# Low parts of a split-float kernel made by VectorE alone behind attention, instead of by VectorE and GpSimd

## The chip, the core and the metric

The kernel runs on one core of a Trainium2 chip. Its time is the device time in microseconds of one execution; three runs of the kernel before gave 2046.16, 2047.84 and 2050.9 us, a median of 2047.84 us. The engines are named as in the profile: PE (TensorE), PEld (its weight load), DVE (VectorE), ACT (ScalarE), POOL (GpSimd) and SP (SyncE, which issues most DMAs).

## The reference

Three stages follow each other. The input is q, k, v of 4 batches x 8 heads x 576 positions x 64 features.

```python
# attention with an exponential feature map
def phi(x):
    proj = np.einsum('bhsd,df->bhsf', x, w_phi)
    proj = proj - np.max(np.abs(proj), axis=-1, keepdims=True)
    return np.concatenate([np.exp(proj), np.exp(-proj)], axis=-1)
...
# first gated layer, 2304 tokens x 512
a = x @ w1; b = x @ w2
x = (a * b @ w3) @ w_out
...
# eight experts, every token goes through all of them
P = np.exp(logits)
for _ in range(8):
    P /= P.sum(1, keepdims=True) + 1e-09
    P /= P.sum(0, keepdims=True) + 1e-09
    P *= N / E
for e in range(E):
    h = np.maximum(x @ w1[e], 0.0)
    out += P[:, e:e + 1] * (h @ w2[e])
```

## The kernel before, in words

**Split numbers.** Every product of the two dense stages is made of three matmuls. Each operand is split into a high part (a copy in the type fp32r, mostly by ACT, `copy`, L96) and a low part (the number minus its high part, `subtract`, L99). `mm3` (L86) then issues high x high, high x low and low x high into one bank of PSUM; L87, L88 and L89 are these three matmuls. So every weight and every activation needs one low part, an elementwise subtraction of two tensors in SBUF.

**Which engine makes which part.** The table `ENG` (L13) gives a letter per step: a is ACT, v DVE, g POOL. A string of several letters is walked through by an index. `Wl="vgg"` (low parts of the experts' w1) has three pieces per tile: the first, 1024 columns wide, goes to DVE, the second (256 columns) and the third (512) to POOL. `W2l="vg"` sends the low parts of w2 to DVE for even units and to POOL for odd ones. `ol="vvvg"` sends two of the eight low parts of the product w3 w_out to POOL. `Xs="gv"` sends the sums of the first 768 columns of X to POOL and those of later columns to DVE. The low part of c = a*b (L717) is written out as a POOL instruction.

**Stages.** Attention takes the first 240 us or so. Then the gated layer runs over six column blocks j of 384 tokens: for each of eight row tiles ft it makes a and b (tiles ab), their product (L715), its high part cH on ACT (L716) and its low part cL (L717), and then four products px with w3 w_out. In the first block (j = 0) the weights w1 and w2 are also rebuilt from 64-bit words (L637 to L646) and split. Between the blocks DVE makes sums of expert weights ahead of time (`sum_next`, `sum_make`, L468).

**The experts.** They run over three super-columns s of 768 tokens. In the first (s = 0) each of the eight experts e has four units (p = 0 to 3) of `unit` (L851): seven products of six matmuls each, in the order a11, s2, s3, s1, a22, a12, s4 (`products`, L819). After each product DVE adds the PSUM bank into the running sums c (L836; ACT copies the first, L834). Five banks are in turn. A unit ends in two `h_split` (L812): hH by ACT, hL by DVE (L815). After the four units come six output tiles py of 24 matmuls (L942), which need all eight hH and hL, and a gated sum on DVE (L956, L958). The weights of the next unit are split meanwhile (`prep_w1`, L529), w2 of this unit behind it (`split_w2`, L792), and for experts 3 to 6 the sums of w2 are made (`sums_w2`, L806). In s = 1 and 2 the split weights are read back from DRAM, and no step of the change occurs there.

**Sinkhorn.** The gate's P is normalised eight times by rows and columns (`sinkhorn_rows`, L881, and `sinkhorn_cols`, L889), in small DVE instructions L883 to L897 and one matmul per round (cs, L891). `between` (L905) issues these steps behind the products of expert 0, so both DVE and PE carry them in their queues between other work.

**What sets the order.** Each engine works through its own queue in order and waits at the head of it. The order in the queues is chosen when the program is built: instructions get priorities (`tc.high_priority(60)` for the adds L836 and for the last h_split), and a scheduler places what is ready by its own idea of durations. Where a step changes its engine, the order of both engines, and of PE behind them, can change.

Of the kernel before, what the change touches and what calls it, by code (L numbers as in the profile page):

```python
# [11 lines left out]

ENG = dict(  # L13
    kh="a", num="a", rc="ga", xmul="gvgg", xh="a", xl="ggvg", woh="a",
    wol="g", w3h="a", w3l="g", w34="aaav", wh="av", wl="v", oh="va", ol="vvvg", Xh="a",
    Xl="v", Xs="gv", Wt="v", Wh="a", Wl="vgg", W2h="a", W2l="vg", Tw="v", Th="a", Tl="v",
)
AF = mybir.ActivationFunctionType
ALU = mybir.AluOpType
# [3 lines left out]
def f32(ap):  # L23
    return ap.bitcast(F32)
# [3 lines left out]
def kernel(  # L28
# [17 lines left out]
    nc = tc.nc  # L46
# [32 lines left out]
    def x_at(p, kt, c0, n):  # L79
        i, o = divmod(c0, NH)  # L80
        return XHL[i][p][:, kt, o : o + n]
# [4 lines left out]
    def mm3(ps, aH, aL, bH, bL, start, stop):  # L86
        nc.tensor.matmul(ps, aH, bH, start=start, stop=False)  # L87
        nc.tensor.matmul(ps, aH, bL, start=False, stop=False)  # L88
        return nc.tensor.matmul(ps, aL, bH, start=False, stop=stop).ins  # L89
# [418 lines left out]
    def load_w1(u):  # L508
        if u < len(units):
            s, e, p = units[u]  # L510
            if s > 0:
                return
            rawW1[u] = rw1.tile([P, 7, 2 * P], F32, name=f"r1_{u}", tag="r")
            nc.sync.dma_start(rawW1[u][:, 4:7], moe2_w1[e, p][:, 1:4])
            nc.sync.dma_start(rawW1[u][:, 0:4], W1T[u])
# [13 lines left out]
    def prep_w1(u):  # L529
        if u >= len(W1S):  # L530
            return
        r = rawW1.pop(u)
        hb, ha = w1_tiles(u)
        for i, (t, c, o) in enumerate(((ha, slice(0, 4), 0), (ha, slice(4, 5), 0), (hb, slice(5, 7), 5))):
            d = slice(c.start - o, c.stop - o)
            copy("Wh", t[:, 0, d], r[:, c], i)
            subtract("Wl", t[:, 1, d], r[:, c], f32(t[:, 0, d]), i)
        for t, d in zip((hb, ha), W1S[u]):
            nc.sync.dma_start(d, f32(t))
# [7 lines left out]
    def sbuf(c, name, bufs=1, side="right"):  # L547
        return c.enter_context(tc.tile_pool(name=name, bufs=bufs, side=side, reuse_waits="tile"))
# [28 lines left out]
    def sum_load(n):  # L577
        if n < len(jobs):
            kind, k = jobs[n]
            rawT[n] = tq[0].tile([P, 4, 2 * P], F32, name=f"tr{n}", tag="tr", bufs=3)  # L580
            if kind == "w1":
                nc.sync.dma_start(rawT[n], moe2_w1[k // NP, k % NP])
            else:
                nc.sync.dma_start(rawT[n].rearrange("p (j h) d -> p j h d", j=2), w2_rows(*k))
# [20 lines left out]
    def sum_next(behind):  # L605
        if made[0] < len(jobs):
            with tc.issue_after(behind):
                sum_make(made[0])
            made[0] += 1

    with ExitStack() as c2:
# [13 lines left out]
        w34 = {}  # L625

        def get_w12(n):
            ft, w = divmod(n, 2)
            if n < NW:
                t = W12E[n]  # L630
            else:
                r = rb.tile([P, DF], U32, name=f"rw{n}", tag="r")
                nc.sync.dma_start(r, w12i[ft][:, w * DM : (w + 1) * DM].bitcast(U32))
                r = r.rearrange("p (n x) -> p n x", x=2)
                t = st2.tile([P, DM], F32, name=f"w{n}", tag="wr")
                u = t.bitcast(U32)
                nc.scalar.activation(t, r[:, :, 1].bitcast(F32), AF.Copy, scale=2.0**-112)  # L637
                nc.vector.tensor_scalar(
                    u, u, 3, 0x7FFFFFFF, ALU.logical_shift_left, ALU.bitwise_and
                )  # L640
                nc.vector.scalar_tensor_tensor(
                    u, r[:, :, 0], 29, u, ALU.logical_shift_right, ALU.bitwise_or
                )
                nc.vector.scalar_tensor_tensor(
                    u, r[:, :, 1], 0x80000000, u, ALU.bitwise_and, ALU.bitwise_or
                )  # L646
            pool = w12a if ft == 0 else w12p
            hi = pool.tile([P, KT, P], F32R, name=f"wH{n}")
            lo = pool.tile([P, KT, P], F32R, name=f"wL{n}")
            t = t.rearrange("p (k f) -> p k f", k=KT)  # L650
            copy("wh", hi, t, n)
            subtract("wl", lo, t, f32(hi), n)
            w12[n] = hi, lo

        def get_w34(i):
            t = st2.tile([P, DM], F32, name=f"wo{i}", tag="wr")
            nc.sync.dma_start(t, W34[i // 2][:, i % 2])
            hi = w34p.tile([P, DM], F32R, name=f"woH{i}")
            lo = w34p.tile([P, DM], F32R, name=f"woL{i}")
            copy("oh", hi, t, i)  # L660
            subtract("ol", lo, t, f32(hi), i)
            w34[i] = hi, lo
# [30 lines left out]
        for j in range(NT // N1):  # L693
            c0 = j * N1
            for ft in range(FT):
                ab = []
                for w in range(2):
                    n = 2 * ft + w
                    if j == 0:
                        for i in range(3) if n == 0 else ():  # L700
                            get_w12(i)
                        if n + 3 < 2 * FT:
                            get_w12(n + 3)
                        if n >= FT:
                            get_w34(n - FT)
                    ps = ab_p.tile([P, N1], F32, name=f"ab{j}_{ft}_{w}", tag="ab")
                    hi, lo = w12[n]
                    for kt in range(KT):
                        mm3(ps, hi[:, kt], lo[:, kt], x_at(0, kt, c0, N1), x_at(1, kt, c0, N1), kt == 0, kt == KT - 1)
                    ab.append(ps)  # L710
                a_sb = ct.tile([P, N1], F32, name=f"a{j}_{ft}", tag="a")
                nc.scalar.copy(a_sb, ab[0])
                h, l = cH[ft], cL[ft]
                cc = a_sb
                behind = nc.vector.tensor_tensor(cc, ab[1], a_sb, ALU.mult).ins  # L715
                nc.scalar.copy(h, cc)  # L716
                nc.gpsimd.tensor_tensor(l, cc, f32(h), ALU.subtract)  # L717
                if 0 < j and (ft < FT - 1 if c0 + N1 < NT else ft % 2 == 0):
                    sum_next(behind)
            if c0 + N1 == NT:  # L720
                assert made[0] == len(jobs)
                c7.close()
                c3.close()
                xt_p.append(sbuf(c2, "xt6", KT))
                xc = sbuf(c4, "xc", side="left")
                wc1 = sbuf(c4, "wc1", 2, "left")
                c6 = c4.enter_context(ExitStack())
                rw1 = sbuf(c6, "rw1", 2, "left")
                wc1c = []
                load_w1(0)  # L730
                load_w1(1)
                prep_x(0)
                prep_w1(0)
            for dt in range(KT):
                ps = px_p.tile([P, N1], F32, name=f"px{j}_{dt}", tag="px")
                dc = slice(dt * P, (dt + 1) * P)
                for ft in range(FT):
                    hi, lo = w34[ft]
                    mm3(ps, hi[:, dc], lo[:, dc], cH[ft], cL[ft], ft == 0, ft == FT - 1)
                xt = xt_p[-1].tile([P, N1], F32, name=f"xt{j}_{dt}", tag="xt")  # L740
                nc.scalar.copy(xt, ps)
                i, o = divmod(c0, 2 * N1)
                nc.sync.dma_start(XS[i][:, dt, o : o + N1], xt)
                xh, xl = x_at(0, dt, c0, N1), x_at(1, dt, c0, N1)
                nc.scalar.copy(xh, xt)
                behind = nc.vector.tensor_tensor(xl, xt, f32(xh), ALU.subtract).ins
                if 0 < j < NT // N1 - 1:
                    sum_next(behind)
            if c0 < NH:
                logits([j])  # L750
            elif c0 + N1 == NT:
                logits(range(NH // N1, NT // N1))
            if j == 0:
                c5.close()
                tq.append(sbuf(c7, "tq", 2))
                for k in range(3):
                    sum_load(k)
            if c0 + N1 == NH:
                cx[0].close()
                rx = sbuf(c4, "rx", side="left")  # L760
                load_x(0)
# [5 lines left out]
    with c4:  # L767
# [238 lines left out]
        for u, (s, e, p) in enumerate(units):  # L1006
# [15 lines left out]
            a = [a01[:, lo_], a01[:, hi_], a2d[:, lo_]]  # L1022
# [135 lines left out]
```

## Time and profile before

| | us |
|---|---|
| median of three runs | 2047.84 |
| the profiled execution's own time | 2048.16 |
| its span, first to last instruction | 2046.4 |
| PE busy | 1994.6 (97%) |
| DVE busy | 1430.8 (70%) |
| ACT busy | 777.5 (38%) |
| POOL busy, 260 instructions | 297.2 (15%) |

The time lies 1.8 us above the span. PE's busy time is made of spans whose ends are modelled: a matmul of 384 columns has a span of some 340 ns, while the next one starts 0.17 to 0.18 us after it. So PE counts as idle only where the gap between two starts is longer than that span, and a busy share of 97% does not say that PE is at its peak. DVE's instructions overlap a little in the same way. POOL is busy until about 1050 us and idle behind it.

### The profile page before, as it was taken

The page shows a single profiled execution, that of the slowest core. Times are in us where ns is not written, and L with a number is a line of the kernel's source. Part 1 is how long each engine was busy: PE and PEld are TensorE (multiplying, and loading weights), DVE is VectorE, ACT ScalarE, POOL GpSimd, SP SyncE. Part 2 cuts the span into 40 slices and gives each one's busy share as a digit, 9 for nine tenths or more (in the row PEclk, how much of TensorE's full clock was granted, in tenths as well). Part 3 has the DMA queues.
Part 4 walks back from the last instruction along what each step waited for, and adds up shares of the span by engine and source line. Part 5 has one row for each costly group of instructions (what it writes and reads, how often), then busy time and mean ns, then how long its engine had stood idle before and what let it go on. Part 6 is the DMA issues. An engine that isn't in the chain of part 4 may idle for free.

```text
span 2046.4 us, 34054 instructions
## 1 busy us (share of the span) xinstructions
PE 1994.6 (97%) x13605; PEld 1865.1 (91%) x13605; DVE 1430.8 (70%) x2320; ACT 777.5 (38%) x1435; POOL 297.2 (15%) x260
## 2 busy tenths in 40 slices
PE   7899999999989999999999999999999999999999
PEld 6677789999988888888889999999999999999999
DVE  7766766666686459766776666777768677776666
ACT  6666532323433224332343333343334334333333
POOL 3433321121322223312220000000000000000000
PEclk9999999999999999999999999999999999999999
DMA  6433248788587668988976666666668666666664
GB/s 213 143 135 117 92 136 264 269 291 279 189 306 277 242 263 287 323 310 299 336 285 226 250 246 246 248 250 248 243 252 309 247 245 251 250 241 250 249 252 150
DMA packets 155502, 496.79 MB, mean 243 GB/s; under 512 B 12624, under 2 KB 73936, under 8 KB 128464
## 3 DMA queue, kind: packets, MB, share of 16 engines
q1 hardware_dynamic: 154752, 493.96, 67.5%
q8 instruction: 107, 1.75, 0.3%
q10 hardware_dynamic: 592, 0.66, 0.1%
q14 instruction: 51, 0.42, 0.1%
HBM read 348.82 MB, written 145.75 MB: 242 GB/s over the span
## 4 chain that ended last, share of the span: by engine, by line
PE 77%; DVE 9%; ACT 4%; issue 4%; DMA 3%; POOL 3%; SPq 0%; ACTq 0%; POOLq 0%; DVEq 0%
PE ps L87 5%; PE ps L89 5%; PE ps L88 5%; PE py L89 4%; PE pa L87 4%; PE pa L88 4%; PE pa L89 4%; PE py L88 4%; PE py L87 4%; PE b L1041 3%; PE b L1040 3%; PE b L1039 3%; PE ab L89 2%; PE ab L87 2%; PE ab L88 2%
## 5 line engine op out<-in xcount | busy, mean ns | idle before, releaser
L836 DVE TENSOR_TENSOR c<-c,ps 128x384 f32<-128x384 f32 x480 | 255.3, 547 | 58.3 <-PE ps L89 53.7
L834 ACT COPY c<-pa 128x384 f32<-128x384 f32 x96 | 45.7, 476 | 360.4 <-PE pa L89 321.8
L89 PE MATMUL py<-w,hL 128*128 128x512 f32 x384 | 153.8, 401 | 2.4 <-DVE hL L815 2.4
L87 PE MATMUL py<-w,hH 128*128 128x512 f32 x384 | 152.5, 397 | 2.9 <-ACT hH L814 2.8
L88 PE MATMUL py<-w,hH 128*128 128x512 f32 x384 | 152.4, 397 | 0.0
L1058 DVE SCALAR_TENSOR_TENSOR o<-mt,Pw,o 128x512 f32<-128x512 f32 x84 | 58.3, 747 | 122.7 <-ACT mt L1048 122.7
L99 POOL TENSOR_TENSOR w<-r,w 128x256 fp32r<-128x256 f32 x64 | 93.1, 1469 | 342.7 <-ACT w L96 307.9
L87 PE MATMUL ab<-XH,wH 128*128 128x384 f32 x384 | 131.3, 342 | 4.2 <-DVE wH L96 2.2
L89 PE MATMUL ab<-XH,wL 128*128 128x384 f32 x384 | 131.2, 342 | 1.5 <-DVE wL L99 1.5
L88 PE MATMUL ab<-XL,wH 128*128 128x384 f32 x384 | 130.4, 340 | 0.0
L958 DVE SCALAR_TENSOR_TENSOR o<-py,Pw,o 128x512 f32<-128x512 f32 x42 | 31.4, 748 | 125.8 <-PE py L89 125.8
L836 DVE TENSOR_TENSOR c<-c,pa 128x384 f32<-128x384 f32 x192 | 102.8, 548 | 9.8 <-PE pa L89 8.8
L1039 PE MATMUL b<-t,dh 128*128 128x256 f32 x384 | 108.7, 283 | 0.0
L1040 PE MATMUL b<-t,dh 128*128 128x256 f32 x384 | 108.7, 283 | 0.0
L1041 PE MATMUL b<-t,dl 128*128 128x256 f32 x384 | 108.7, 283 | 0.0
L89 PEld LDWEIGHTS py<-w,hL 128*128 128x128 f32 x384 | 72.2, 188 | 24.4 <-DVE hL L815 7.6
L993 ACT ACTIVATE c<-c 128x384 f32<-128x384 f32 x64 | 33.6, 526 | 156.1 <-DVE c L836 156.1
L87 PEld LDWEIGHTS py<-w,hH 128*128 128x128 f32 x384 | 72.4, 188 | 21.2 <-ACT hH L814 4.7
L717 POOL TENSOR_TENSOR cL<-a,cH 128x384 fp32r<-128x384 f32 x48 | 56.8, 1183 | 231.2 <-ACT cH L716 231.2
L88 PEld LDWEIGHTS py<-w,hH 128*128 128x128 f32 x384 | 72.3, 188 | 17.2 <-DVE w L99 0.3
L815 DVE SCALAR_TENSOR_TENSOR hL<-c,hH 128x768 fp32r<-128x768 f32 x64 | 79.8, 1254 | 3.1 <-ACT hH L814 2.5
L96 ACT CAST w<-r 128x512 fp32r<-128x512 f32 (+2 forms) x96 | 61.9, 686 | 45.4 <-issue 31.5
(266 smaller groups left out, 6493.7 us busy)
## 6 DMA issues: line engine op xcount, KB each, us to landing
t<-w2s SPq DMA_DIRECT2D x112, 1024.0 KB, 4.7
w<-w1s SPq DMA_DIRECT2D x64, 1280.0 KB, 5.5
w1s<-w SPq DMA_DIRECT2D x32, 1280.0 KB, 7.4
w<-w1s SPq DMA_DIRECT2D x64, 512.0 KB, 5.0
tr<-in_moe_w_dram SPq DMA_DIRECT2D x48, 512.0 KB, 5.4
w2s<-w SPq DMA_DIRECT2D x96, 256.0 KB, 4.3
w1t<-tt SPq DMA_DIRECT2D x32, 512.0 KB, 6.2
r<-w1t SPq DMA_DIRECT2D x32, 512.0 KB, 7.3
```

Source lines behind the costliest of these rows:

```text
L87: nc.tensor.matmul(ps, aH, bH, start=start, stop=False)
L88: nc.tensor.matmul(ps, aH, bL, start=False, stop=False)
L89: return nc.tensor.matmul(ps, aL, bH, start=False, stop=stop).ins
L96: (e.copy if e is nc.scalar else e.tensor_copy)(out, src)
L99: engine(key, i).tensor_tensor(out, a, b, ALU.subtract)
L717: nc.gpsimd.tensor_tensor(l, cc, f32(h), ALU.subtract)
L815: nc.vector.scalar_tensor_tensor(hL[ft], src, 0.0, f32(hH[ft]), ALU.max, ALU.subtract)
L836: nc.vector.tensor_tensor(o, t, ps, ALU.add)
L1039: nc.tensor.matmul(dst[i], H[:, c], T[:, 0], start=f, stop=False, skip_group_check=True)
L1040: nc.tensor.matmul(dst[i], H[:, c], T[:, 1], start=False, stop=False, skip_group_check=True)
L1041: nc.tensor.matmul(dst[i], L[:, c], T[:, 0], start=False, stop=l, skip_group_check=True)
L1058: nc.vector.scalar_tensor_tensor(o, src[i], w, o, ALU.mult, ALU.add)
```

## The change

Five strings of `ENG` lose their letter g, and the low part of c (L717) is issued on DVE. Nothing else is edited; no operation is added or left out, and the operands stay the same.

```diff
-    wol="g", w3h="a", w3l="g", w34="aaav", wh="av", wl="v", oh="va", ol="vvvg", Xh="a",
-    Xl="v", Xs="gv", Wt="v", Wh="a", Wl="vgg", W2h="a", W2l="vg", Tw="v", Th="a", Tl="v",
+    wol="g", w3h="a", w3l="g", w34="aaav", wh="av", wl="v", oh="va", ol="v", Xh="a",
+    Xl="v", Xs="v", Wt="v", Wh="a", Wl="v", W2h="a", W2l="v", Tw="v", Th="a", Tl="v",
...
-                nc.gpsimd.tensor_tensor(l, cc, f32(h), ALU.subtract)
+                nc.vector.tensor_tensor(l, cc, f32(h), ALU.subtract)
```

What moves from POOL to DVE: 48 low parts of c (384 columns each), 32 pieces of w1 of 512 and 32 of 256 columns, 16 low parts of w2 (1024 columns), 2 low parts of w3 w_out (512 columns) and the 4 sums of the first X (768 columns): 134 instructions. What POOL does in attention stays.

The first place is DVE's queue in the third and fourth unit of expert 4 (units 18 and 19, first super-column). c_8371 and c_8452 are the sums of units 18 and 19, w_19_5 and w_19_2 the two tiles of unit 19's w1, w_18_8433 w2 of unit 18, hL_6077 and hL_6081 the low parts of unit 18's h.

```order
 L836 TENSOR_TENSOR c_8371<-c_8371,pa_8405 128x384
 L836 TENSOR_TENSOR c_8371<-c_8371,pa_8413 128x384
 L836 TENSOR_TENSOR c_8371<-c_8371,ps_8423 128x384
+L99 TENSOR_TENSOR w_19_5_8362<-r_19_8277,w_19_5_8362 128x256
+L99 TENSOR_TENSOR w_19_2_8361<-r_19_8277,w_19_2_8361 128x512
+L815 SCALAR_TENSOR_TENSOR hL_6077<-c_8371,hH_6069 128x768
+L815 SCALAR_TENSOR_TENSOR hL_6081<-c_8371,hH_6073 128x768
+L836 TENSOR_TENSOR c_8452<-c_8452,ps_8461 128x384
+L99 TENSOR_TENSOR w_18_8433<-r2b,w_18_8433 128x2x512
+L836 TENSOR_TENSOR c_8452<-c_8452,ps_8469 128x384
 L99 TENSOR_TENSOR w_20_5_8443<-r_20_8358,w_20_5_8443 128x1024
```

The two pieces of unit 19's w1 that POOL made now stand behind the last add of unit 18, ahead of that unit's hL, and the low part of unit 18's w2 comes later than it did.

The second place is PE's queue at the start of expert 4's output tiles. py_0 and py_1 are the first two tiles, hH_6070 and hL_6078 the parts of h of the fourth unit's first half, hH_6074 and hL_6082 those of its second half.

```order
 L89 MATMUL py_0_8520<-w_18_8433,hL_6081 128x512
 L87 MATMUL py_0_8520<-w_19_8514,hH_6070 128x512
-L88 MATMUL py_0_8520<-w_19_8514,hH_6070 128x512
-L89 MATMUL py_0_8520<-w_19_8514,hL_6078 128x512
-L87 MATMUL py_0_8520<-w_19_8514,hH_6074 128x512
-L88 MATMUL py_0_8520<-w_19_8514,hH_6074 128x512
-L89 MATMUL py_0_8520<-w_19_8514,hL_6082 128x512
 L87 MATMUL py_1_8546<-w_16_8261,hH_6067 128x512
 L88 MATMUL py_1_8546<-w_16_8261,hH_6067 128x512
```

The last five matmuls of the first tile now stand nine matmuls of the second tile later.

The third place is DVE's queue in expert 0, where the rounds of Sinkhorn are interleaved with the units. L897 ends one half round, L883 to L887 are the next; w_1_6303 is w2 of unit 1, w_3_5 and w_3_2 are the tiles of unit 3's w1.

```order
+L897 TENSOR_TENSOR Pw<-Pw,ri 128x144
+L99 TENSOR_TENSOR w_1_6303<-r2a,w_1_6303 128x2x512
+L883 TENSOR_REDUCE rs<-Pw 128x18
 L99 TENSOR_TENSOR w_3_5_6314<-r_3_6200,w_3_5_6314 128x1024
+L884 TENSOR_SCALAR rs<-rs 128x18
+L99 TENSOR_TENSOR w_3_5_6314<-r_3_6200,w_3_5_6314 128x256
+L886 RECIPROCAL rri<-rs 128x18
+L99 TENSOR_TENSOR w_3_2_6313<-r_3_6200,w_3_2_6313 128x512
+L887 TENSOR_TENSOR Pw<-Pw,rri 128x144
+L815 SCALAR_TENSOR_TENSOR hL_6077<-c_6323,hH_6069 128x768
```

Three of the former POOL pieces now stand between the small instructions of this half round, where adds and an hL stood before.

## Rows read from the trace of the kernel before

**Rows 1.** The page, part 4: the chain that ended last, by engine.

```profile
PE 77%; DVE 9%; ACT 4%; issue 4%; DMA 3%; POOL 3%; SPq 0%; ACTq 0%; POOLq 0%; DVEq 0%
```

**Rows 2.** Windows: us of stretch, then each engine's busy time (count), PEclk, DMA.

```profile
242.00:248.00 6.00, 5.41 (x22) 5.41 (x23) 6.00 (x12) 3.09 (x6) 1.28 (x1) 0.72 0.08 26
300.00:550.00 250.00, 249.06 (x1417) 245.79 (x1417) 147.51 (x270) 75.39 (x134) 52.30 (x43) 1.00 0.75 255
550.00:610.00 60.00, 53.01 (x284) 47.18 (x284) 54.50 (x98) 25.66 (x41) 22.15 (x14) 0.97 0.77 283
610.00:1030.00 420.00, 412.75 (x2011) 361.17 (x2010) 279.27 (x403) 135.74 (x191) 104.42 (x62) 1.00 0.81 291
1075.00:2046.00 971.00, 966.84 (x6792) 962.63 (x6790) 690.11 (x1167) 343.40 (x647) 0.00 (x0) 1.00 0.68 245
```

**Rows 3.** Waits of PE, 235 to 1080 us: waiter <- releaser: total us, times, longest.

```profile
PE cs L891 <- DVE Pw L887: 6.3, 5, 1.5
PE py L87 <- ACT hH L814: 2.8, 3, 1.0
PE py L89 <- DVE hL L815: 2.4, 5, 0.8
PE ab L87 <- DVE wH L96: 2.2, 3, 1.4
...
PE ps L87 <- DVE c L836: 1.4, 4, 0.4
...
PE lg L678 <- DVE XL L746: 0.9, 1, 0.9
```

**Rows 4.** Groups of POOL: out<-in, shape, xcount | busy us, mean ns | idle before.

```profile
L717 POOL TENSOR_TENSOR cL<-a,cH 128x384 fp32r<-128x384 f32 x48 | 56.8, 1183 | 231.2 <-ACT cH L716 231.2
L99 POOL TENSOR_TENSOR w<-r,w 128x512 fp32r<-128x512 f32 x32 | 53.0, 1656 | 25.5 <-ACT w L96 25.5
...
L99 POOL TENSOR_TENSOR w<-r2b,w 128x1024 fp32r<-128x1024 f32 x9 | 25.5, 2838 | 11.5 <-ACT w L96 11.3
```

**Rows 5.** Groups of DVE, 235 to 1080 us, while POOL works.

```profile
L815 DVE SCALAR_TENSOR_TENSOR hL<-c,hH 128x768 fp32r<-128x768 f32 x64 | 79.8, 1254 | 3.1 <-ACT hH L814 2.5
...
L99 DVE TENSOR_TENSOR w<-r,w 128x1024 fp32r<-128x1024 f32 x32 | 46.8, 1463 | 0.0
...
L641 DVE SCALAR_TENSOR_TENSOR w<-rw,w 128x512 uint32<-128x512 uint32 x11 | 11.5, 1049 | 0.1
...
L99 DVE TENSOR_TENSOR woL<-wo,woH 128x512 fp32r<-128x512 f32 x6 | 4.0, 686 | 0.1
```

**Rows 6.** Groups of DVE, 1080 to 2046 us, POOL idle.

```profile
L982 DVE SCALAR_TENSOR_TENSOR bl<-c,bh 128x768 fp32r<-128x768 f32 x64 | 61.0, 953 | 8.2 <-ACT bh L981 8.2
...
L998 DVE TENSOR_TENSOR c<-c 128x384 f32<-128x384 f32 x64 | 35.4, 553 | 0.6
```

**Rows 7.** Timeline of DVE in expert 4: start us, us, instruction.

```profile
833.85 0.56 DVE L836 TENSOR_TENSOR c<-c,ps 128x384 f32<-128x384 f32 x1 [1.40 <-PE ps L89]
...
835.92 0.42 DVE L468 TENSOR_TENSOR r2a<-r2a 128x256 f32<-128x256 f32 x1
836.26 1.01 DVE L836 TENSOR_TENSOR c<-c,ps 128x384 f32<-128x384 f32 x2
...
838.45 1.22 DVE L99 TENSOR_TENSOR w<-r,w 128x1024 fp32r<-128x1024 f32 x1
...
842.92 2.72 DVE L815 SCALAR_TENSOR_TENSOR hL<-c,hH 128x768 fp32r<-128x768 f32 x1
...
865.95 1.82 DVE L815 SCALAR_TENSOR_TENSOR hL<-c,hH 128x768 fp32r<-128x768 f32 x2
```

**Rows 8.** Timeline of POOL, the same stretch.

```profile
842.21 2.61 POOL L99 TENSOR_TENSOR w<-r2b,w 128x1024 fp32r<-128x1024 f32 x1
```

**Rows 9.** Timeline of DVE in expert 0: one small Sinkhorn instruction, twice.

```profile
573.85 0.17 DVE L884 TENSOR_SCALAR rs<-rs 128x18 f32<-128x18 f32 x1
...
596.47 2.06 DVE L884 TENSOR_SCALAR rs<-rs 128x18 f32<-128x18 f32 x1
```

## The prediction

> **What bounds the kernel now.** I read the chain that ended last first: 77% of it is PE, 9% DVE, 4% ACT, 3% POOL [rows 1]. So a POOL instruction taken away is worth nothing by itself; it counts where PE waits for something that POOL delays. The windows by stage come second [rows 2]: behind attention PE is idle 0.9 us of 250 in the gated layer, 7.0 of 60 at the start of the experts, 7.2 of 420 in the experts up to 1030 us, and 4.2 of 971 behind that, where POOL and the change have no work. DVE is full at two places: 6.00 of 6 us in the first block of the gated layer, 54.5 of 60 at the start of the experts. Third, what PE waits for [rows 3]: 6.3 us for Pw, five times; 6.6 us in the units and output tiles (2.8 for hH, 2.4 for hL, 1.4 for a bank that the adds c free, twelve waits); 2.2 us for wH of the first block; 0.9 us for the last XL. Nearly every releaser is DVE, or an ACT instruction fed by DVE. Attention comes before the change and keeps its instructions.
>
> **Why DVE is late there.** The same subtraction of 768 columns takes 1254 ns on DVE while POOL works [rows 5] and 953 ns when POOL is idle [rows 6]. One case is seen whole: hL starts at 842.92 us and takes 2.72 us, up to 845.64, while a POOL subtraction runs from 842.21 to 844.82 [rows 7, 8]; 0.82 us after POOL's end the DVE instruction is done. A Sinkhorn instruction of 18 columns takes 0.17 us or 2.06 us [rows 9]. Adds that read PSUM are not drawn out: two of them take 1.01 us [rows 7]. So DVE instructions on SBUF stand still while POOL holds its operands. I take that as the mechanism, since the cover is one to one.
>
> **What the change adds to DVE**, at undisturbed durations: 48 low parts of c at 553 ns [rows 6], 26.5 us; 32 pieces of w1 at 686 ns [rows 5], 22.0; 32 pieces at 0.42 us (same width, L468) [rows 7], 13.4; 16 low parts of w2 at 1.22 us [rows 7], 19.5; four sums of X at 953 ns [rows 6], 3.8; two of w_out at 686 ns, 1.4. Sum 86.6 us. On POOL a c part took 1183 ns, a piece of w1 1656, one of w2 2838 [rows 4].
>
> **What comes back.** Three groups of rows 5 alone give 64 x 0.301 + 32 x 0.243 + 11 x 0.363 = 31.1 us (against 953, 1220 and 686 ns). POOL's own busy time in the middle three stretches, 52.3 + 22.2 + 104.4 = 178.9 us [rows 2], is the upper bound. So DVE's sum moves by something between +55 and -92 us. I take about zero, a return of some 86 us, nearer to the lower end: more groups than these three work on SBUF, but a POOL instruction in whose time DVE has nothing to do there costs nothing. DVE was idle 102 us of 250 and 141 us of 420 [rows 2], so the sum is not what decides; the full places are.
>
> **Experts 1 to 7, units and output tiles.** In expert 4 DVE works from 833.85 to 867.77 us, 33.9 us, from the first add to the last hL [rows 7]. One instruction starts some 0.08 us before the end of the one in front, as the two adds of 1.01 us show. So steps are 0.46 us for an add, 0.87 for hL, 1.14 for 1024 columns, 0.61 for 512, 0.34 for 256. In the order before there stand 28 adds (12.9), 8 hL (7.0), 6 instructions of 1024 columns (6.8) and 6 of 256 (2.0) between these ends: 28.7 us, so some 5 us were standstill. In the new order there are 28 adds, 8 hL, 6 of 1024, 3 of 512 (1.8) and 5 of 256 (1.7): 30.2 us. PE's 168 matmuls need 168 x 0.176 = 29.6 us (249.06 us for 1417 [rows 2]). DVE ends 3.7 us earlier than before, though it does 1.5 us more. A new wait would be the 256-column piece of unit 19, which stands behind unit 18's last add: PE's first matmul that needs it stands nine matmuls, 1.6 us, behind the start of that unit in the new order, and the piece is done 0.46 + 0.34 us behind the last product. At the output tiles the five matmuls that need the last hL were also moved behind nine others, some 2 us. A wait costs PE more than its idle time: a matmul's span ends 0.17 us after the next start, so twelve waits of 6.6 us are 8.6 us. Bounds: all of it goes, or none, if DVE stands 3.7 us for ACT's high parts instead. I take the first, less a rest of 1.0: **-7.6 us**.
>
> The Trainium skill, VectorE: DVE Perf Modes, section The DRAIN you can't avoid, says that the next operation does not start until the pipeline is empty, and adds that one that is not held starts earlier. By its first half each of the 50 steps would be 0.08 us longer, 34.2 us for expert 4, and nothing would be won there; the two adds in 1.01 us of rows 7 show the second half.
>
> **Sinkhorn in expert 0.** PE waited 6.3 us for Pw, 7.1 with five times 0.17 [rows 3], behind small instructions that were held up as in rows 9. These standstills go. In exchange the former POOL pieces stand in the chain: in the round shown 1.14 + 0.34 + 0.61 = 2.1 us come in, and two hL and two adds, 2.7 us, go out. Bounds: all 7.1 us gone, or 6.1 us more (four units' extra pieces of w1 at 0.95 and two of w2 at 1.14), if PE had nothing else to do meanwhile. The new order of PE puts twelve matmuls of the output tiles into the fourth unit, so I take the first, less a rest of 2.1: **-5.0 us**.
>
> **First block and last XL.** In the full first block eight c parts and two of w_out come in, 10 steps, 8 x 0.47 + 2 x 0.61 = 5.0 us, of which PE could see all; L641 alone gives 11 x 0.363 = 4.0 us back [rows 5] and its neighbours more. Between +1 and -2.2 (the wait for wH), I take **-1.0 us**. XL of the last block stood behind POOL pieces of w1, 0.9 us and 0.17: **-1.0 us**. The other blocks of the gated layer are covered by PE, which is idle 0.9 us there; a c part on DVE is done sooner than POOL's 1183 ns. The X sums are needed only when the experts start and shorten from POOL's pace: nothing. POOL issues no DMA that the change moves; stores and loads of w1 follow its low parts, which are ready earlier. The span of 2046.4 us loses 14.6 us, and 1.8 us around it stay: 2033.6 us against the profiled run's 2048.16, and 0.3 less against the median: **2033 us**.
>
> **Rivals.** First, nothing measurable: the places of DVE's waits are taken by the next late, above all ACT's hH, which is already 2.8 of the 6.6 us, and the pieces in the Sinkhorn chain. For it speaks that ACT's instructions are queued behind the same adds; against it that PE has its own reserve of about 2 us in the new order. If hH takes over the waits of hL and c, and Pw keeps its own, 2 us of the sum remain: 2046 us.
>
> Second, slower: DVE becomes the bound in every expert. It has 30.2 us of steps against PE's 29.6, and 12 splitting steps instead of 6, each of which waits at the head of the queue for ACT's high part while the adds that free PE's banks stand behind it. It decides from 3.7 us of such waiting per expert; at 6 us, 2.3 us are lost per expert, 16 us in seven, the 7.6 us don't come, and the other places give their 7.0: 2048 + 16 - 7 = 2057 us. Against it stands that the order of ACT keeps the high parts of w1 and w2 one unit ahead. The Trainium skill, Perfetto Trace Analysis, section Optimizing Scalar/DVE Operations, is on its side: with DVE saturated, giving work to GpSimd may make sense. It adds that the two share a port, so that it might not help; rows 7 and 8 bear out the second sentence.
>
> Third, more: every wait of rows 3 goes, 16.0 us and 21 times 0.17, and with the waits of the first block the granted clock's dip there (1.2 GHz for a part, 0.72 of full speed over 6 us) [rows 2], 0.28 x 6 = 1.7 us: 2048 - 21 = 2027 us. Against it stands that the waits behind attention's own POOL instructions stay.
>
> **How the numbers follow.** The forecast has 0.65, with a range of its own from 2028 to 2041; nothing measurable 0.14; slower 0.08; more 0.13. A change of this kernel's time can be told from 0.2% on, 4.1 us: faster is below 2043.7, slower above 2051.9. Forecast and more give 0.78; a few in a hundred of the first rival also lie below 2043.7, so faster 0.80, same 0.12, slower 0.08. The range 2025 to 2045 leaves out the slower case, the worse half of the first rival and the end of the third.
>
> **What would show it.** hL (L815) at a mean of 950 to 960 ns instead of 1254, the 1024-column pieces of w1 near 1220 and L884 near 0.17 throughout: the standstills are gone. PE's waits for hH, hL and a c bank below 1 us together, and for Pw below 2 us. In the first block DVE still full, but shorter. DVE's busy time within some 15 us of 1430.8. Wrong would be: hL still long without POOL (then something else holds it), PE waiting for ACT's hH as before, or new waits of PE for w1's low parts at unit starts and of DVE for ACT's high parts.

## The result, and the profile after

The changed kernel takes 2019.9 us (median of four, 2018.8 to 2020.8), the kernel before beside it 2048.8 (2046.2 to 2050.9). The ratio is 0.9865, 95% interval 0.9853 to 0.9876: 28.9 us less. The forecast was 2033 us, 2025 to 2045. The direction was right, and the experiments below bear out the cause; the gain is nearly twice the 15 us that were forecast, and the time lies below the range.

The page, parts 1 and 4, of the changed kernel (busy time, share, instructions; then the chain that ended last, as [rows 1]):

```profile
PE 1987.1 (98%) x13605; PEld 1867.6 (93%) x13605; DVE 1426.9 (71%) x2454; ACT 779.6 (39%) x1435; POOL 92.4 (5%) x126
...
PE 87%; DVE 5%; ACT 3%; POOL 2%; DMA 2%; issue 1%; SPq 0%; ACTq 0%; POOLq 0%; DVEq 0%
```

DVE is busy 3.9 us less than the 1430.8 us of before, with 86.6 us of work more. In the chain PE has ten points more; DVE, ACT, "issue", DMA and POOL have them less.

The groups of DVE behind attention, to hold against [rows 5] and [rows 9]:

```profile
L815 DVE SCALAR_TENSOR_TENSOR hL<-c,hH 128x768 fp32r<-128x768 f32 x64 | 59.9, 951 | 0.3
L99 DVE TENSOR_TENSOR w<-r,w 128x1024 fp32r<-128x1024 f32 x32 | 39.0, 1219 | 0.4 <-ACT w L96 0.4
...
L717 DVE TENSOR_TENSOR cL<-a,cH 128x384 fp32r<-128x384 f32 x48 | 26.6, 554 | 5.4 <-ACT cH L716 5.4
...
L641 DVE SCALAR_TENSOR_TENSOR w<-rw,w 128x512 uint32<-128x512 uint32 x11 | 7.6, 687 | 0.0
...
L884 DVE TENSOR_SCALAR rs<-rs 128x18 f32<-128x18 f32 x8 | 1.4, 172 | 0.0
```

hL went from 1254 to 951 ns, the 1024-column piece from 1463 to 1219, L641 from 1049 to 687, the small Sinkhorn instruction from 718 to 172 in the mean. The trace also tells the hL apart one by one: in the kernel before 15 of the 64 overlap no GpSimd instruction, and they take 950 ns in the mean; the other 49 take 1347.

All waits of PE from 235 to 1064 us (waiter <- releaser: total us, times, longest), as [rows 3]:

```profile
PE ab L89 <- DVE wL L99: 1.4, 2, 0.9
PE px L87 <- DVE woH L96: 1.2, 1, 1.2
PE ab L87 <- ACT wH L96: 1.0, 1, 1.0
PE lp L684 <- DVE lgs L680: 0.2, 1, 0.2
PE ab L87 <- DVE wH L96: 0.2, 1, 0.2
```

Four us are left, 3.8 of them in the first block. Pw, hH, hL and the bank that the adds c free are gone.

Windows of the changed kernel (columns as [rows 2]); each stage now begins some us earlier:

```profile
242.00:248.00 6.00, 5.40 (x22) 5.40 (x23) 6.00 (x14) 3.11 (x6) 0.00 (x0) 0.72 0.19 59
300.00:550.00 250.00, 249.95 (x1426) 247.43 (x1425) 150.17 (x317) 79.27 (x141) 0.00 (x0) 1.00 0.76 257
550.00:610.00 60.00, 59.64 (x325) 53.00 (x324) 54.58 (x136) 25.04 (x40) 0.00 (x0) 1.00 0.93 343
610.00:1030.00 420.00, 420.00 (x2093) 376.62 (x2092) 296.62 (x476) 149.42 (x206) 0.00 (x0) 1.00 0.83 298
```

PE's idle time went from 7.0 to 0.4 us in 550 to 610 and from 7.2 to 0.0 in 610 to 1030. The first window has not changed: DVE full, clock 0.72.

Stages, from the first matmul of each to the first of the next (us, one profiled execution each):

| stage | before | after | c | X, w_out | w1 | w2 |
|---|---|---|---|---|---|---|
| first block | 64.83 | 61.46 | 63.13 | 63.46 | 64.72 | 64.69 |
| blocks 2 to 6 | 256.76 | 255.27 | 255.35 | 255.26 | 256.13 | 256.21 |
| last logits, expert 0, units of expert 1 | 111.85 | 100.90 | 112.00 | 108.76 | 106.03 | 108.92 |
| output tiles of expert 1 to the end of expert 7, first products behind | 451.84 | 440.56 | 451.43 | 456.38 | 448.38 | 445.54 |

The third stage ends at the first matmul of expert 1's output tiles (py); below, it is called expert 0 for short, and the fourth experts 1 to 7. Before and after have the same number of matmuls in each. The last four columns are the first four experiments.

### The profile page after: what moved, and what is told of

Its sections match the earlier page's. It is cut to its first block, busy times and chain, and to the rows that moved or that the text cites. A ratio compares the mean times of both kernels' runs of the same rounds, so it can differ in the third digit from the quotient of the medians.

```text
span 2018.9 us, 33841 instructions
## 1 busy us (share of the span) xinstructions
PE 1987.1 (98%) x13605; PEld 1867.6 (93%) x13605; DVE 1426.9 (71%) x2454; ACT 779.6 (39%) x1435; POOL 92.4 (5%) x126
## 4 chain that ended last, share of the span: by engine, by line
PE 87%; DVE 5%; ACT 3%; POOL 2%; DMA 2%; issue 1%; SPq 0%; ACTq 0%; POOLq 0%; DVEq 0%
PE ps L87 6%; PE ps L89 6%; PE ps L88 6%; PE pa L87 5%; PE pa L89 5%; PE pa L88 5%; PE py L89 4%; PE py L88 4%; PE py L87 4%; PE b L1041 3%; PE b L1040 3%; PE b L1039 3%; PE ab L89 3%; PE ab L87 3%; PE ab L88 3%; PE a L1039 2%
## 5 line engine op out<-in xcount | busy, mean ns | idle before, releaser
L96 ACT CAST w<-r 128x1024 fp32r<-128x1024 f32 (+2 forms) x96 | 63.8, 690 | 71.7 <-PE pa L89 27.1
L87 PEld LDWEIGHTS ab<-XH,wH 128*128 128x128 f32 x384 | 72.6, 189 | 2.9 <-ACT wH L96 1.3
L99 DVE TENSOR_TENSOR w<-r,w 128x512 fp32r<-128x512 f32 (+2 forms) x96 | 72.5, 774 | 3.2 <-ACT w L96 3.0
L89 PEld LDWEIGHTS ab<-XH,wL 128*128 128x128 f32 x384 | 72.5, 189 | 2.1 <-DVE wL L99 2.1
```

The costliest lines, as they stand in the source:

```text
L96: (e.copy if e is nc.scalar else e.tensor_copy)(out, src)
L99: engine(key, i).tensor_tensor(out, a, b, ALU.subtract)
```

## The experiments

**Theory**: GpSimd instructions that read SBUF hold up DVE's SBUF instructions, DVE is late, PE waits. **Rival 1**: the new order of the queues brings the gain. **Rival 2**: GpSimd's own results came late. Each ratio is against the kernel before, run beside it, with its 95% interval.

**One part of the change at a time.** The change is made of four strings of `ENG`, not five (`Wl`, `W2l`, `Xs`, `ol`), and the line L717. From the kernel before, only the low parts of c:

```
-                nc.gpsimd.tensor_tensor(l, cc, f32(h), ALU.subtract)
+                nc.vector.tensor_tensor(l, cc, f32(h), ALU.subtract)
```

> The kernel before with only the low parts of c and the last block's woL unit moved from GpSimd to VectorE; w1, w2, the X sums and the last low parts of w_out stay on GpSimd. Theory (GpSimd's reads of SBUF hold VectorE's SBUF instructions back, TensorE then waits): the c waits of the experts (1.4 us) and the waits for cL and cH in the gated layer's blocks go, hL stays drawn out at about 1254 ns because w1 and w2 still run on GpSimd: 2040 to 2046 us, 2 to 8 us below before. Rival (VectorE's queue order brings the gain): the order in experts barely changes, so again about 2045. Rival (GpSimd's own lateness): only the wait for cL goes, 2047.

The kernel that ran moves the 48 low parts of c and nothing else; woL of the last block, which the expectation names, stays on GpSimd. Measured 2045.1 us (ratio 0.9982, 0.9973 to 0.9992). The gain stands in the first block (-1.7) and blocks 2 to 6 (-1.4); hL stayed at 1226 ns. The waits for the adds c in the experts, which were expected to go, did not: 1.6 us against 1.4.

Only w1 (`Wl="v"`):

> The kernel before with only the w1 low pieces moved to VectorE. Theory: in each expert the GpSimd work falls from w1 + w2 + c to w2 + c, the first half of each unit is undisturbed; the experts' 14.6 us of gain (11.3 in experts 1 to 7, 3.3 in expert 0) comes by about half: 2036 to 2042 us. Rival (order): the w1 pieces stand ahead of more in VectorE's queue, all of the order's gain comes here: 2030 or below. Rival (GpSimd's lateness): w1L never was late, so 2047 to 2049.

Measured 2037.2 (0.9946, 0.9931 to 0.9961). hL fell to 947 ns. Before, w1 pieces overlap hL for 30.3 us in all and w2 pieces for 16.4; here the w2 pieces, still on GpSimd, overlap it for only 1.8, so the new order keeps them away as well.

Only w2 (`W2l="v"`):

> The kernel before with only the odd w2 low pieces moved to VectorE. Theory: about half of the experts' gain, with the Sinkhorn steps (which lie beside w2 and w1 pieces of expert 0) at least partly still held: 2036 to 2043 us, hL mean about 1100 ns. Rival (order): 2030 or below, or as before. Rival (GpSimd's lateness): 2047 to 2049.

Measured 2039.6 (0.9957, 0.9942 to 0.9971), hL 1110 ns, PE's waits for Pw 3.5 us instead of 6.3.

Only the X sums and w_out (`Xs="v", ol="v"`):

> The kernel before with only the first X sums and the last low parts of w_out moved to VectorE. Theory: the wait for XL at the last logits (0.9 us) and some of the dip of the granted clock behind it (1.7 us) go, the experts stay as they were: 2043 to 2047 us. Rival (order): 2047. Rival (GpSimd's lateness): the X sums were late by the 0.9 us of that wait alone: 2046.

Measured 2045.8 (0.9985, 0.9976 to 0.9995). The waits for XL and xt are gone. The profiled run lost in the experts what it had won before them: PE waited 3.4 us for the adds c instead of 1.4, and from 929 to 933 us the granted clock fell to 0.50, behind waits for hH and hL of 1.4 us that the kernel before has too, without a fall.

All four times are within what the theory expected; the gains 3.0, 11.0, 8.5 and 2.3 add up to 24.8 of the 28.9 us. Lateness as the cause falls for w1 and w2, where it had 2047 to 2049; order isn't excluded by these four.

**GpSimd's reads put back, with the new order.** In the changed kernel GpSimd again reads the high parts, into a scratch tile:

```
+            if i > 0:
+                for q in range(d.start, d.stop):
+                    x = f32(t[:, 0, q])
+                    nc.gpsimd.tensor_tensor(junk, x, x, ALU.subtract)
...
+            if u % 2:
+                for q in range(4):
+                    x = f32(hi[:, q // 2, q % 2 * 2 * P : (q % 2 + 1) * 2 * P])
+                    nc.gpsimd.tensor_tensor(junk, x, x, ALU.subtract)
```

> The changed kernel, VectorE's order as it is there, and beside it GpSimd again makes subtractions in the experts, of 256 columns each, from the rounded high parts that it read before (w1 all but the first four row groups, every second w2 unit), into a scratch tile that nobody reads. Theory (GpSimd's reads hold VectorE back): hL goes from 951 to 1150 to 1260 ns, w1 pieces from 1219 to above 1350, the Sinkhorn steps and TensorE's waits for hL, hH and Pw come back: 2036 to 2050 us. Rival (VectorE's order brought the gain): 2018 to 2022, as the order stays. Rival (GpSimd's results came late): nobody waits for these results, 2018 to 2022.

And as its control, writes at the same places (`copy` of one element, then `memset(junk, 0.0)` two or three times):

> The changed kernel with GpSimd at the same places setting a scratch tile to zero (instructions that write SBUF and read none of it), after a copy of one element per partition of the same high part. Theory in its narrow form (what holds VectorE back are GpSimd's reads): hL stays within 20 ns of 951, 2018 to 2023 us. In its wide form (any GpSimd access to SBUF): hL above 1050, 2025 to 2045. Rivals (order, lateness): 2018 to 2022.

Groups of the kernel with reads:

```profile
L824 DVE SCALAR_TENSOR_TENSOR hL<-c,hH 128x768 fp32r<-128x768 f32 x64 | 63.5, 1007 | 0.0
...
L100 DVE TENSOR_TENSOR w<-r,w 128x256 fp32r<-128x256 f32 x32 | 17.2, 537 | 1.2 <-ACT w L97 1.2
...
L542 POOL TENSOR_TENSOR junk<-w 128x256 f32<-128x256 f32 x96 | 111.8, 1165 | 615.8 <-ACT w L97 610.8
L807 POOL TENSOR_TENSOR junk<-w 128x256 f32<-128x256 f32 x64 | 54.3, 848 | 15.8 <-ACT w L97 11.2
```

And of the one with writes:

```profile
L824 DVE SCALAR_TENSOR_TENSOR hL<-c,hH 128x768 fp32r<-128x768 f32 x64 | 59.9, 952 | 0.5
...
L100 DVE TENSOR_TENSOR w<-r,w 128x256 fp32r<-128x256 f32 x32 | 13.4, 418 | 2.9 <-ACT w L97 2.9
...
L542 POOL MEMSET junk<- 128x256 f32 x128 | 40.0, 313 | 7.5
L540 POOL COPY junk<-w 128x1 f32<-128x1 f32 x64 | 39.0, 610 | 658.5 <-ACT w L97 657.0
```

Reads: 2030.0 us (0.9909, 0.9894 to 0.9924). Writes: 2020.9 (0.9868, 0.9851 to 0.9884), as the changed kernel. The two have the same order on PE, and on DVE but for one w2 piece that changes places with a small instruction. In the kernel with writes 29 of the 64 hL have a memset beside them, and these take 953 ns in the mean, so the writes do not merely fall elsewhere. So 100 us of GpSimd beside DVE cost nothing while they write, and 166 us cost 9 to 10 us when they read, though nobody waits for the values. (ACT waits for GpSimd to leave a buffer, 6.8 us in all with reads and 4.7 with writes.) That speaks against both rivals. But the theory expected 2036 to 2050 and hL above 1150: here the reads hit DVE's w pieces (256 columns 537 ns instead of 418) more than hL, and most of the loss lies in the third stage (108.2 us against 100.5), part of it a fall of the clock (mean 0.90 over the 35 us from 540 to 575, so 3.5 us, against 1.00 in the kernel with writes).

The Trainium skill, SBUF — State Buffer, section Who interferes with whom, says that a DVE instruction with two SBUF inputs contends with a GpSimd instruction that reads SBUF, and not with one that only writes. These two kernels agree: hL 1007 and 952 ns.

**The old shapes, and the same cut short.** In the changed kernel GpSimd subtracts in place, in the raw weights, behind DVE:

```
+            if i > 0:
+                nc.gpsimd.tensor_tensor(r[:, c], r[:, c], f32(t[:, 0, d]), ALU.subtract)
...
+            if u % 2:
+                t = RW[u % len(RW)]
+                nc.gpsimd.tensor_tensor(t, t, f32(W2[p][0]), ALU.subtract)
```

> The changed kernel with VectorE's and TensorE's order as there, and GpSimd making again each w1 and w2 subtraction that it made before, in the shapes of before (256, 512 and 1024 columns), into the raw weights once VectorE is done with them; nobody waits for the values. Theory (what counts is GpSimd's time in reads, and longer instructions hold VectorE back for longer than the 256-column ones of the run before): hL above 1150 ns, 2038 to 2046 us. Rival (order, with GpSimd's reads adding only what the 256-column run showed): 2027 to 2032. Rival (lateness): 2018 to 2022.

> The same subtractions as in the kernel before this one in the list, cut into instructions of 256 columns. Theory (held by the length of each instruction): hL about 1000 to 1050 ns, 2026 to 2034 us, clearly below the uncut form. Rival (held by the amount read, whatever the length): within 2 us of the uncut form.

Of the sixteen w2 subtractions only eight are made in these two kernels, since the others' raw tiles take another path; w1 has all. Uncut: 2052.6 us (1.0020, 1.0010 to 1.0029), hL 1317 ns. Cut to 256 columns: 2044.3 (0.9983, 0.9973 to 0.9994), hL 1195. Both lost more than expected, and cutting takes away 8 of 33 us: the length of one GpSimd instruction counts, but it is the smaller part. In both kernels the next raw weights are loaded only when GpSimd is done with the old ones (SP waits 19.6 us in all for its w2 subtractions in the uncut kernel, 33.4 in the cut one). That did not reach DVE: it waits 1.7 us for ACT's high parts of the weights in either, 4.9 in the changed kernel.

One place shows it. DVE at the end of expert 1's units in the changed kernel (start us, us, instruction):

```profile
654.72 1.02 DVE L99 TENSOR_TENSOR w<-r,w 128x256 fp32r<-128x256 f32 x2
655.66 1.82 DVE L815 SCALAR_TENSOR_TENSOR hL<-c,hH 128x768 fp32r<-128x768 f32 x2
657.39 1.22 DVE L99 TENSOR_TENSOR w<-r2b,w 128x1024 fp32r<-128x1024 f32 x1
```

and the same three in the uncut kernel, with GpSimd beside them:

```profile
662.79 1.02 DVE L99 TENSOR_TENSOR w<-r,w 128x256 fp32r<-128x256 f32 x2
663.73 2.36 DVE L820 SCALAR_TENSOR_TENSOR hL<-c,hH 128x768 fp32r<-128x768 f32 x2
666.00 2.28 DVE L99 TENSOR_TENSOR w<-r2b,w 128x1024 fp32r<-128x1024 f32 x1
...
663.71 3.49 POOL L539 TENSOR_TENSOR r<-r,w 128x256 f32<-128x256 f32 x2 [7.19 <-ACT hH L819]
```

Without a gap on DVE the same three take 5.5 us instead of 3.9, from the first start to the last end. PE stood at that place for the w2 piece; waits of this kind were its largest in the uncut kernel:

```profile
PE py L88 <- DVE w L99: 12.1, 6, 2.4
PE ps L87 <- DVE c L841: 3.0, 4, 1.2
PE cs L896 <- DVE Pw L892: 2.5, 4, 1.1
```

So the new order with GpSimd's reads is no faster than the kernel before, by 0.1 to 0.3% even slower. DVE has the 86.6 us more there, which is the likely reason.

**The old order without reads.** The kernel before, with GpSimd setting its low parts of w1, w2, c and the last w_out to zero:

```
+        if key in ("Wl", "W2l", "ol") and engine(key, i) is nc.gpsimd:
+            nc.gpsimd.memset(f32(out), 0.0)
+            return
...
-                nc.gpsimd.tensor_tensor(l, cc, f32(h), ALU.subtract)
+                nc.gpsimd.memset(f32(l), 0.0)
```

> The kernel before, with its order of instructions on VectorE and TensorE in the experts, but GpSimd sets the low parts it makes of w1, w2, c and the last w_out to zero instead of subtracting (it leaves these low terms out of the result); the four X sums stay on GpSimd. Theory (reads of GpSimd, not order): without reads hL is 951 and the waits of the experts are gone, 2017 to 2024 us, though VectorE keeps its old order and does 85 us less. Rival (order brought the gain): 2040 to 2048.

Its groups, and all its waits of PE of 0.2 us or more, 235 to 1093 us:

```profile
L818 DVE SCALAR_TENSOR_TENSOR hL<-c,hH 128x768 fp32r<-128x768 f32 x64 | 60.5, 953 | 2.6 <-ACT hH L817 2.5
...
L720 POOL MEMSET cL<- 128x384 f32 x48 | 19.6, 420 | 220.6 <-PE px L88 216.9 <-POOL cL L720 0.4
...
PE ab L87 <- ACT wH L96: 1.5, 1, 1.5
PE ab L89 <- DVE wL L102: 0.9, 1, 0.9
PE px L87 <- ACT woH L96: 0.6, 1, 0.6
PE px L89 <- DVE woL L102: 0.4, 1, 0.4
```

2023.0 us (0.9876, 0.9861 to 0.9890). PE's order in experts 1 to 7 is that of before to the last matmul (in expert 0 the Sinkhorn matmuls cs stand up to six places elsewhere), and no wait is left in the experts: rival 1 falls. The stages are 61.1, 255.4, 101.4 and 440.3 us, those of the changed kernel to 0.5 us. This kernel alone would not exclude lateness, as a memset waits for no high part; the reads whose values nobody uses do.

**How much room DVE has.** The changed kernel, the first w1 piece of each unit made twice:

```
+            if i == 0:
+                subtract("Wl", t[:, 1, d], r[:, c], f32(t[:, 0, d]), i)
```

> The changed kernel with the 1024-column low piece of each w1 unit made twice by VectorE, 4 x 1.22 = 4.9 us more in each expert, 39 us in all. Theory (VectorE has room in the experts, its share there is about 0.78): 2018 to 2024 us. Rival (VectorE was near to being the bound in each expert, as the forecast's rival had it from 3.7 us more on): 2028 to 2055.

2028.7 us (0.9904, 0.9889 to 0.9919), 8.8 more than the changed kernel. The number is at the lower edge of the rival's, and outside the theory's 2018 to 2024; the place is not the rival's. PE's order changed here too, and some matmuls crossed the boundary of the stages, so lateness is compared, that is how much later than the median step of their kind PE's matmuls start: the third stage is 4.8 us later than in the changed kernel, part of it a fall of the clock at 561 us, and experts 1 to 7 with the first products 1.9, which is one wait, in the last expert. PE's only wait from 662 to 1072 us:

```profile
PE py L87 <- DVE o L960: 1.9, 1, 1.9
```

Four times 1.22 us fit into the later experts but for that wait; where Sinkhorn and the last logits lie, they do not.

**Attention's low parts too.** To `wol="v", w3l="v"`, and then also `xl="v"`:

> The changed kernel with attention's low parts of w_out and w3 (24 subtractions of 512 columns, 30.7 us on GpSimd, 24 x 0.68 = 16.4 us on VectorE) moved to VectorE too. Theory: wL in the first block falls from 822 to 684 ns and the waits for woH, wH and wL of 3.8 us behind attention shrink to about 2, the dip of the granted clock there (1.7 us) may go; VectorE is 0.68 to 0.80 busy in attention, so 16 us more fit: 2014 to 2021 us. Rival (VectorE is what attention waits for, as kv <- e and pp <- d show): attention gets longer by up to 16 us, 2022 to 2035.

> As the kernel before this one in the list (attention's low parts of w_out and w3 on VectorE), and the low parts of x in attention too (16 subtractions of 576 columns, 23.1 us on GpSimd, about 16 x 0.77 = 12.3 us on VectorE). Theory: as there or a little better, 2012 to 2022 us. Rival (VectorE sets attention's pace): 28.7 us more VectorE work in 235 us that it fills to 171 us, most of it before a wait of TensorE: 2028 to 2045.

2021.4 us (0.9870, 0.9855 to 0.9884) and 2021.8 (0.9873, 0.9858 to 0.9887): no gain over the changed kernel. In the first, wL behind attention stayed at 820 ns, where 684 was expected, and PE's waits there did not shrink (3.9 us against 3.8). In the second, wL of the first 300 us fell from 918 to 755 ns and the first block took 60.9 us instead of 61.5 (298.35 less 237.43), but attention ended 1.9 us later. No version here beats the changed kernel.

## Why the prediction was right and wrong

Right: hL 951 ns (950 to 960 foretold), 1024 columns 1219 (1220), L884 172 (0.17 us); PE's waits for hH, hL and c below 1 us and for Pw below 2; DVE's busy time within 15 us of before; the first block still full on DVE. DVE's waits for ACT's high parts of the weights grew from 0.8 to 4.9 us, and PE waited for none of them in the experts. That DVE's sum came out near zero was a choice between bounds of 31 and 179 us of return, not a working; 90.5 came back. "One to one" was read from one case: over all hL of the kernel before, 46.7 us beside GpSimd cost 19.5 us, 0.42 us for each. In expert 4 DVE needs from 815.12 to 846.27, 31.2 us, where 30.2 was the sum of its steps. The two rows behind that:

```profile
815.12 0.56 DVE L836 TENSOR_TENSOR c<-c,ps 128x384 f32<-128x384 f32 x1 [1.43 <-PE ps L89]
...
844.45 1.82 DVE L815 SCALAR_TENSOR_TENSOR hL<-c,hH 128x768 fp32r<-128x768 f32 x2
```

Wrong was the size, and the step that failed is the sum of what PE's waits cost. Its terms against the stages:

| term | forecast | measured |
|---|---|---|
| experts 1 to 7 | -7.6 | -11.3 |
| Sinkhorn in expert 0 | -5.0 | -7.6 |
| last XL | -1.0 | -3.3 |
| first block | -1.0 | -3.4 |
| other blocks of the gated layer | 0 | -1.5 |
| rest | 0 | -0.4 |
| span | -14.6 | -27.5 |

(The third stage of the table above is split by lateness: last XL is that of the matmuls up to 570.0 us before and 563.2 after, Sinkhorn the rest. The split is good to 0.1 us.)

*Experts 1 to 7.* That a wait costs its idle time and 0.17 us held for the wait itself: the twelve cost 8.6 us from start to start, as forecast. But the step behind a wait is slow too, and a wait shorter than 0.17 us is in no list. PE in the kernel before, at a wait for hH and one for hL:

```profile
801.06 0.50 PE L87 MATMUL py<-w,hH 128*128 128x512 f32 x1 [0.81 <-ACT hH L814]
801.39 0.40 PE L88 MATMUL py<-w,hH 128*128 128x512 f32 x1
802.19 0.50 PE L89 MATMUL py<-w,hL 128*128 128x512 f32 x1 [0.40 <-DVE hL L815]
802.53 0.40 PE L87 MATMUL py<-w,hH 128*128 128x512 f32 x1
802.76 0.39 PE L88 MATMUL py<-w,hH 128*128 128x512 f32 x1
803.06 0.50 PE L89 MATMUL py<-w,hL 128*128 128x512 f32 x1
```

From 801.06 and from 802.19 to the next start are 0.33 and 0.34 us, where an undisturbed step takes 0.23 (802.53 to 802.76). The view of waits lists no wait at the step from 802.76 to 803.06, and yet it is 0.07 longer, and the step behind it, to the next output matmul, 0.10. Of such steps, 0.07 us or more above the median and not in the list of waits, there were 28, 3.0 us in all; two are left, 0.2. The forecast had none of them, and kept back a rest of 1.0 that didn't come: 8.6 + 3.0 - 0.2 = 11.4, and 11.3 was measured.

*Sinkhorn.* All 7.2 us of the five waits went (7.1 in the forecast); the rest of 2.1 that was kept back for the w1 and w2 pieces in the chain did not appear. At the fourth cs of the changed kernel Pw was done at 586.95 us and PE came to it at 587.30; the twelve matmuls moved ahead of it take 2.8 us (12 x 0.234), so without them PE would have waited there.

*Last XL.* The waits for xt, which the forecast left out, and for XL cost 1.9 us with their starts, and behind them the granted clock fell, in the kernel before:

```profile
560.00:564.60 4.60, 2.70 (x18) 1.39 (x17) 4.35 (x6) 1.15 (x3) 2.54 (x2) 1.00 1.00 402
564.60:568.00 3.40, 3.40 (x13) 3.36 (x12) 0.92 (x3) 0.48 (x1) 0.00 (x0) 0.50 0.99 270
568.00:572.00 4.00, 4.00 (x24) 3.65 (x23) 2.50 (x5) 1.05 (x1) 0.00 (x0) 1.00 1.05 403
```

PE had been idle 1.9 of 4.6 us; then it ran 3.4 us at 1.2 GHz instead of 2.4, which is 1.7 us. In the changed kernel the clock is whole there. The fall does not follow such waits each time: the kernels with only c and with only w2 on DVE have the same two waits; with w2 it falls at 565 us too, with c it stays whole. So the 1.7 us are sure for this execution alone. The kernel with only c:

```profile
540.00:575.00 35.00, 31.90 (x183) 28.34 (x182) 27.20 (x39) 17.64 (x30) 11.68 (x7) 1.00 0.81 288
```

The rival "more" counted a fall of the clock, but at the first block, where it stayed.

*First block.* c alone took 1.7 us off and w_out with the X sums 1.4; together they passed the better bound, -2.2. The ten steps that came in on DVE cost less than the standstills that went: DVE is busy 49.0 us of the first block with 92 instructions, 49.6 with 82 before.

*Other blocks.* The forecast put nothing here, because PE covers them. PE's 0.9 idle us were one place, with 1.3 us from start to start: a cL of GpSimd and two DVE sums drew each other out (DVE first, then GpSimd), and the last a, cH and cL came late.

```profile
439.60 1.57 DVE L468 TENSOR_TENSOR tt<-tr,tt 128x256 f32<-128x256 f32 x2
441.09 0.55 DVE L715 TENSOR_TENSOR a<-ab,a 128x384 f32<-128x384 f32 x1
...
439.30 1.58 POOL L717 TENSOR_TENSOR cL<-a,cH 128x384 fp32r<-128x384 f32 x1 [2.77 <-ACT cH L716]
442.26 1.00 POOL L717 TENSOR_TENSOR cL<-a,cH 128x384 fp32r<-128x384 f32 x1 [1.37 <-ACT cH L716]
```

So where the forecast chose between bounds, kept a rest back or put nothing, the chip gave the far end or more: 2.4 us in the first block, 1.5 in the other blocks, the rests of 1.0 and 2.1. With the slow steps, 3.0, and the clock and the wait for xt, some 2.3, these are 12.3 of the 12.9 us missed. The rival "nothing measurable" fell: PE waits for hH no more, though ACT does the same work. The slower rival fell too, and its point of 3.7 us of waiting per expert was too low: 4.9 us more of DVE work in each cost 1.9 us in all in experts 1 to 7.

Open is why 256-column reads of one operand twice (hL 1007 ns) hold hL back less than those of two operands (1195). How much lies beside hL does not explain it: 32.5 us of overlap cost 3.8 there, 0.12 us for each, and 48.8 cost 15.8 here, 0.32 for each. No run separates the operands from what else differs.

## What to carry to other kernels

Work that reads SBUF on GpSimd is not free where DVE is the feeder of PE: compare the mean of one DVE shape with GpSimd busy and idle, and if they differ clearly, as 1254 and 953 ns here, price the work on DVE at its undisturbed time. A wait of PE costs its idle time, the slow step behind it and at times a fall of the clock: sum PE's starts against its median step in a stage, not the list of waits alone. Here many small waits had one cause, and with the cause nearly all of them went; rests kept back for caution made the forecast too small.

## What the chip showed that was not expected

- GpSimd writing SBUF (memset, 313 ns for 256 columns) leaves DVE alone, hL 952 ns; GpSimd reading it does not, 1007 to 1317 ns.
- The same reads in shorter instructions cost less: 2044.3 against 2052.6 us. The Trainium skill, SBUF — State Buffer, section Who interferes with whom, says of DVE's two-port modes that whoever issues first keeps the shared ports for its whole instruction; it does not say so of instructions with two SBUF inputs, as these are. The 8 us go that way, and the 24 that the cut form still loses show that short ones hold DVE back too.
- The hold-up is mutual: in the kernel with reads a GpSimd subtraction of 256 columns took 613 ns in the mean where DVE worked on SBUF operands for less than a twentieth of its time (31 of them), and 1221 where for more than half (110); cL of 384 columns took 1.00 or 1.58 us.
- The granted clock falls behind waits, but not behind the same waits each time, and the place moves: 3.4 us from 564.6 us before, 6.8 us from 797.2 with only w1 on DVE (mean 0.95 from 770 to 840), 3.4 us between 920 and 940 with only the X sums and w_out, none from 540 to 575 with only c. The kernel before spreads over 4.7 us in its four runs, the changed one over 2.0.
